# Scan and adapter mixture on one core: stores in rows over four units, a written order for every engine, 36 output slots

## The chip, the cores and the metric

One Trainium2 chip, one core. The metric is the device time of one execution in microseconds. Engines are named as in the profile: PE (TensorE matmul), PEld (its weight load), DVE (VectorE), ACT (ScalarE), POOL (GpSimd), SP (SyncE, which only issues DMAs here).

## What is computed

Inputs: a and b of 8 x 6400 x 128 (float32), gate weights 128 x 8, and eight adapters A (128 x 16) and B (16 x 128). First a scan over the 6400 steps of each of the 8 sequences, then on each of the 51200 rows a mixture of the two adapters with the largest gate logits:

```python
for t in range(S):
    h = a[:, t] * h + b[:, t]
    out[:, t] = h
...
logits = x @ w_gate
topk = np.argpartition(-logits, K, axis=1)[:, :K]
...
z = x[mask] @ A[e]
delta[mask] += w[mask, k, None] * (z @ B[e])
...
return x + delta
```

w is the softmax of the two selected logits. The output is 51200 x 128 float32, 26.2 MB, and a and b are 26.2 MB each.

## The kernel before

The 51200 rows are cut into 100 units of 512 rows. Loads bring two units of one input at a time (512 KB, 4 KB to a partition; four loads bring one), into a ring of eight slots for a and one for b. The slots of a are shifted by one unit, so that an a pair is units 1-2, 3-4 and so on, and a b pair 2-3, 4-5. For one unit, numbered v or w in the code:

- AB (PE): transposes of a into the bank pA (one buffer) and of b into pB (two), 64 x 64 pieces in float32; for units 0, 1 and 99 some of it in 128 x 128 pieces, as A and AB apart.
- aev (ACT): copies pA to a_st. scan (DVE): the scan along the free axis, from a_st and pB to xT in float16, a ring of 16 units. Sequences that begin within a unit cut a scan in two.
- L (PE): logits into a part of the bank pTL. Gating works on groups of one to four units: lev (ACT) copies the logits out, then m1, p1, p2, p3, m2, p4 to p7 (m1 and m2 on DVE, the others on GpSimd; the first three groups sort with max on DVE and may have p-steps there), and sig (ACT), which gives the weights g.
- Z (PE): x times all eight A, into pZ (two buffers). mul: the product of Z and g into zw, on DVE from PSUM or, at units 6, 10 and so on to 86, on GpSimd behind an evacuation zev by ACT.
- T (PE): transposes of zw into pTL, the bank of L. tev (ACT): evacuation to zwT.
- R (PE): x through an identity matrix into pO (two buffers), then D (PE): zwT times B on top. oev: evacuation to outt, on ACT, for the last ten units on ACT or DVE.
- st (SP): store from outt, a ring of 24 slots of one unit, two units at a time where these form a pair, so that a partition holds 8 consecutive rows, 4 KB. To get there, R and D take the x and zw of a pair in steps of 8 rows: `x_rows` reads every eighth column of xT, `evacuated` writes a tev with the rows of a pair dealt out. R of a pair therefore waits for both scans and D for both evacuations (`mates`). Units 0, 1 and 96 to 99 are stored singly in 2 KB rows.

The order on each engine is made in `_Plan.schedule`: a list scheduler at build time that goes through the operations by estimated costs and by keys (unit plus an offset by kind). A store is held until scan u0 + 22 (`HOLD`). In the DMA queue of SP, loads go by their unit, a and b in turn. An operation on a shared bank ("TL" of T, tev, L and lev; "A") waits for the last one of the other engine there. Seven matmuls on zeros (`heat`) run ahead of the first load, three more (`fill`) behind the first transposes.

Of the kernel before, what the change touches and what calls it, by code (L numbers as in the profile page):

```python
# [5 lines left out]
ALU = mybir.AluOpType  # L6
ACTF = mybir.ActivationFunctionType
F32 = mybir.dt.float32
# [4 lines left out]
KEY = {  # L13
    "AB": -228.9, "aev": 79.1, "scan": 140.1, "L": -12.2, "lev": -63.6, "gate": 83.5, "sig": 69.7, "Z": 27.8,
    "mul": -75.3, "zev": 6.2, "T": -117.7, "tev": 38.1, "R": 189.8, "D": 29.2, "oev": 168.4,
}
SLACK = {"pe": 20.0, "dve": 20.0, "act": 0.0, "pool": 60.0, "sp": 120.0}
# [3 lines left out]
POOL_MULS = (2, 10, 4, 2)  # L21
# [3 lines left out]
WIDE = 100  # L25
SOLO = (2, 4)
FUSE = (100, 100)
WIDE8 = 460.0
RING = 8
XR = 16  # L30
NOUT = 24
TAIL = 10
FILLS = 1


class _Op:


    def __init__(self, name, engs, kind, unit, cost, emit, deps, dma, bank, mode):
        self.name = name  # L40
        self.engs = engs
        self.eng = engs[0]
        self.kind = kind
        self.unit = unit
        self.cost = cost
        self.emit = emit
        self.deps = deps
        self.dma = dma
        self.bank = bank
        self.mode = mode  # L50
        self.signal = False
        self.done = None
# [7 lines left out]


# [30 lines left out]
class _Plan:  # L92


    def __init__(self, sems, offset, slack):
        self.sems = sems
        self.offset = offset
        self.slack = slack
        self.ops = {}
        self.order = {e: [] for e in sems}  # L100

    def add(self, name, eng, kind, unit, cost, emit, deps=(), dma=None, bank=None, mode=None):

        engs = (eng,) if isinstance(eng, str) else eng
        cost = cost if isinstance(cost, dict) else {e: cost for e in engs}
        self.ops[name] = _Op(name, engs, kind, unit, cost, emit, list(deps), dma, bank, mode)

    def schedule(self, first, link, landing, switch):
        ops = self.ops
        users = {n: [] for n in ops}  # L110
        left = {}
        for op in ops.values():
            op.deps = [ops[d] for d in dict.fromkeys(op.deps) if d in ops]
            left[op.name] = len(op.deps)
            op.key = op.unit + self.offset.get(op.kind, 0.0)
            op.quick = min(c[0] for c in op.cost.values())
        for op in ops.values():
            for d in op.deps:
                users[d.name].append(op)
        begin, end = {}, {}  # L120
        cand = {e: [] for e in self.sems}
        free = {e: first for e in self.sems}
        bank = {}
        mode = None
        for op in ops.values():
            if not left[op.name]:
                for e in op.engs:
                    cand[e].append((0.0, op))
        todo = len(ops)
        while todo:  # L130
            found, soonest = [], {}
            for e, c in cand.items():
                for x in c:
                    op = x[1]
                    t = max(free[e], x[0])
                    if op.bank:
                        for o in bank.get(op.bank, {}).values():
                            if o.eng != e:
                                t = max(t, end[o.name])
                    if op.mode and mode and op.mode != mode:  # L140
                        t = max(t, free[e] + switch)
                    t += op.cost[e][0] - op.quick
                    found.append((t, op, e, x))
                    if t < soonest.get(e, 1e18):
                        soonest[e] = t
            e0 = min(soonest, key=soonest.get)
            limit = soonest[e0] + self.slack.get(e0, 0.0)
            t, op, e, pick = min((f for f in found if f[2] == e0 and f[0] <= limit), key=lambda f: (f[1].key, f[0]))
            t -= op.cost[e][0] - op.quick
            for x in op.engs:  # L150
                cand[x].remove(pick)
            op.eng = e
            mode = op.mode or mode
            if op.bank:
                held = bank.setdefault(op.bank, {})
                op.deps += [o for o in held.values() if o.eng != e]
                held[e] = op
            self.order[e].append(op)
            begin[op.name] = t
            free[e] = t + op.cost[e][0]  # L160
            if op.dma:
                ready = free[e] + 1000.0
                wait = max(0.0, link - ready)
                link = max(link, ready) + op.dma[2]
                end[op.name] = link + 300.0 + min(wait, landing(link))
            else:
                end[op.name] = t + op.cost[e][1]
            todo -= 1
            for u in users[op.name]:
                left[u.name] -= 1  # L170
                if not left[u.name]:
                    for x in u.engs:
                        cand[x].append((max(end[d.name] for d in u.deps), u))
        self.begin, self.end = begin, end
        self.span = max(end.values())
        for op in ops.values():
            for d in op.deps:
                d.signal = True
        for e, seq in self.order.items():
            n = 0  # L180
            for op in seq:
                if op.dma:
                    op.done = op.dma[:2]
                else:
                    n += op.signal
                    op.done = (self.sems[e], n)
# [18 lines left out]
def bass_associative_scan_2x2__then__mixture_of_adapters_kernel(  # L205
# [20 lines left out]
    lo, hi, every, at = POOL_MULS  # L226
    ON_POOL = lambda v: lo < v < NU - hi and v % every == at
# [22 lines left out]
    with ExitStack() as stack:  # L250
# [15 lines left out]
        A_e = sb(nc.sbuf_tensor("A_e", [E, D * R], F32))  # L266
        xT = sb(nc.sbuf_tensor("xT", [128, XR * UT], F16))
        zw = [sb(nc.sbuf_tensor(f"zw{i}", [128, Q, 128], F16)) for i in range(2)]
        zwT = [sb(nc.sbuf_tensor(f"zwT{i}", [128, 2 * UT], F16)) for i in range(2)]
# [26 lines left out]
        s_cst = sb(nc.semaphore("s_cst"))  # L296
        dma_sem = {}

        plan = _Plan(sems, KEY, SLACK)
        add = plan.add  # L300

        def add_dma(name, eng, unit, starts, slot, time, deps=()):
# [11 lines left out]
            add(name, eng, "dma", unit, (450.0 * len(starts), 0.0), emit, deps, (sem, value, time))  # L314


        add("id0", "pool", "fix", -109, (200.0, 450.0), lambda h: h.memset(ident_f[:, :], 0.0))
# [3 lines left out]
            "fix",  # L321
            -109,
            (300.0, 400.0),
# [9 lines left out]
            ["id0"],  # L333
        )

        def cst_load(name, dst, src, after):

            sem = sb(nc.semaphore(f"s_{name}"))
            add(
                name,  # L340
                "act",
                "fix",
                -109,
                (450.0, 0.0),
                lambda h: h.dma_start(dst, src).then_inc(sem, 16),
                after,
                (sem, 16, 100.0),
            )
# [9 lines left out]
        add("w0", "dve", "fix", -109, (60.0, 200.0), lambda h: h.memset(warm[:, :], 0.0))  # L358
        add("table", "act", "fix", -108, (1500.0, 1600.0), lambda h: h.activation(warm[:, :], warm[:, :], ACTF.Sigmoid), ["w0"])
        add("wt", "dve", "fix", -109, (270.0, 400.0), lambda h: h.memset(warm_t[:, :], 0.0))  # L360
# [6 lines left out]
        add("heat", "pe", "fix", -109, (372.0 * HEATS, 372.0 * HEATS), heat, ["wt"], mode="half")  # L367

        def fill(w):


            def emit(h):
                for _ in range(3):
                    last = h.matmul(pO[1][:, :], warm_t[:, 0:128], warm_t[:, :])
                return last

            add(f"fill{w}", "pe", "fix", 1000.0, (600.0, 800.0), emit, [f"AB{w}"])

        for w in range(FILLS):
            fill(w)  # L380
        add("idh", "dve", "fix", -108, (150.0, 330.0), lambda h: h.tensor_copy(ident_h[:, :], ident_f[:, :]), ["id"])
        add("cstg", "pool", "fix", -108, (190.0, 290.0), lambda h: h.tensor_copy(wg_h, cst_f[:, 0:E]), ["ld_g"])
        add(
            "cstA",
            "pool",
            "fix",
            -107,
            (290.0, 390.0),
            lambda h: h.tensor_copy(Acat_h, cst_f[:, E : E + 128]),
            ["ld_A"],  # L390
        )
        add(
            "cstB",
            "pool",
            "fix",
            -106,
            (290.0, 390.0),
            lambda h: h.tensor_copy(Bcat_h, cst_f[:, E + 128 : E + 256]),
            ["ld_B"],
        )  # L400

# [525 lines left out]
```

## Time and profile before

| what | us |
|---|---|
| runs, median of 3 (lowest to highest) | 204.45 (204.28 to 204.6) |
| the profiled execution | 204.28 |
| its span, first to last instruction | 202.5 |
| PE busy | 191.0 |
| DVE busy | 184.7 |
| ACT busy | 174.0 |
| POOL busy | 115.7 |

The span is what the profile shows; 1.78 us of the execution lie around it. Matmuls are pipelined, so PE's busy time is not work at its peak; how long a stage of PE takes is read from start to start in its timeline. In a row of groups, the number behind x is the count, then busy time, mean ns of one, and the idle time just before with what ended it. A DMA row gives KB of one and the time from issue to landing. The granted clock of TensorE was 1.00 throughout.

### The profile page before, as it was taken

The page shows a single profiled execution, that of the slowest core. Times are in us where ns is not written, and L with a number is a line of the kernel's source. Part 1 is how long each engine was busy: PE and PEld are TensorE (multiplying, and loading weights), DVE is VectorE, ACT ScalarE, POOL GpSimd, SP SyncE. Part 2 cuts the span into 40 slices and gives each one's busy share as a digit, 9 for nine tenths or more (in the row PEclk, how much of TensorE's full clock was granted, in tenths as well). Part 3 has the DMA queues.
Part 4 walks back from the last instruction along what each step waited for, and adds up shares of the span by engine and source line. Part 5 has one row for each costly group of instructions (what it writes and reads, how often), then busy time and mean ns, then how long its engine had stood idle before and what let it go on. Part 6 is the DMA issues. An engine that isn't in the chain of part 4 may idle for free.

```text
span 202.5 us, 8763 instructions
## 1 busy us (share of the span) xinstructions
PE 191.0 (94%) x3594; PEld 171.4 (85%) x3594; DVE 184.7 (91%) x268; ACT 174.0 (86%) x383; POOL 115.7 (57%) x244
## 2 busy tenths in 40 slices
PE   7888988899999999999999999999999999999982
PEld 3666777789899999999999999999999999998981
DVE  1699989999999999999999999999999999988970
ACT  2366775969999999999999999999999999999882
POOL 1325337668467565656746656565674687865620
PEclk9999999999999999999999999999999999999999
DMA  7999999999999999999999999999999999988866
GB/s 185 401 408 409 406 408 406 403 406 411 403 413 414 410 419 409 409 411 414 412 416 409 414 413 411 411 415 415 409 412 414 413 414 410 385 350 350 324 271 263
DMA packets 23687, 79.35 MB, mean 392 GB/s; under 512 B 3680, under 2 KB 3808, under 8 KB 23648
## 3 DMA queue, kind: packets, MB, share of 16 engines
q1 hardware_dynamic: 22320, 78.65, 97.3%
q8 instruction: 29, 0.48, 1.0%
q10 hardware_dynamic: 1328, 0.14, 0.5%
q14 instruction: 10, 0.08, 0.1%
HBM read 52.56 MB, written 26.21 MB: 389 GB/s over the span
## 4 chain that ended last, share of the span: by engine, by line
PE 84%; ACT 6%; DVE 5%; issue 2%; POOL 1%; DVEq 0%
PE pA L86 27%; PE pO L82 23%; PE pTL L86 14%; PE pZ L82 10%; PE pTL L82 5%; DVE xT L510 4%; PE pB L86 4%; ACT a_st L491 2%; ACT outt L821 2%; PE pB L82 2%; ACT zwT L786 1%; DVE mx L589 1%; ACT Lg L583 0%; ACT z_sb L715 0%; POOL pn L632 0%
## 5 line engine op out<-in xcount | busy, mean ns | idle before, releaser
L510 DVE TENSOR_TENSOR_SCAN xT<-a_st,xT,pB 128x512 f16<-128x512 f32 x96 | 120.1, 1251 | 3.2 <-ACT zwT L786 0.5
L491 ACT COPY a_st<-pA 128x512 f32<-128x512 f32 x100 | 60.6, 606 | 19.2 <-PE pB L86 14.6
L86 PE MATMUL pA<-ident_f,a_in 64*128 64x64 f32 (+1 forms) x792 | 71.8, 230 | 2.5 <-ACT a_st L491 0.7
L86 PE MATMUL pB<-ident_f,b_in 64*128 64x64 f32 (+1 forms) x792 | 71.9, 230 | 0.3 <-issue 0.2
L86 PEld LDWEIGHTS pA<-ident_f,a_in 64*128 64x128 f32 (+1 forms) x792 | 57.9, 139 | 10.9 <-ACT a_st L491 1.9
L821 ACT COPY outt<-pO 128x512 f32<-128x512 f32 x96 | 59.5, 626 | 1.9 <-PE pO L82 1.7
L786 ACT COPY zwT<-pTL 128x512 f16<-128x512 f16 x95 | 58.4, 615 | 1.0 <-PE pTL L86 1.0
L86 PEld LDWEIGHTS pB<-ident_f,b_in 64*128 64x128 f32 (+1 forms) x792 | 57.5, 138 | 1.0 <-issue 0.7
L729 DVE TENSOR_TENSOR zw<-pZ,g 128x512 f16<-128x512 f32 x79 | 53.2, 679 | 2.4 <-PE pTL L86 1.4
L82 PE MATMUL pO<-ident_h,xT 128*128 128x128 f16 x400 | 40.8, 227 | 0.9 <-ACT outt L821 0.9
L86 PE MATMUL pTL<-ident_h,zw 128*128 128x128 f16 x380 | 37.8, 221 | 0.5 <-ACT zwT L786 0.4
L82 PE MATMUL pZ<-cst_h,xT 128*128 128x128 f16 x400 | 38.1, 219 | 0.0
L82 PE MATMUL pO<-cst_h,zwT 128*128 128x128 f16 x400 | 36.8, 218 | 0.5 <-ACT zwT L786 0.4
L82 PEld LDWEIGHTS pO<-ident_h,xT 128*128 128x128 f16 x400 | 32.5, 147 | 1.5 <-ACT outt L821 1.2
L729 POOL TENSOR_TENSOR zw<-z_sb,g 128x512 f16<-128x512 f32 x21 | 22.3, 1060 | 17.8 <-PE pTL L82 17.3
L82 PE MATMUL pTL<-cst_h,xT 128*128 128x8 f16 x400 | 27.5, 174 | 1.4 <-DVE xT L510 1.3
L82 PEld LDWEIGHTS pZ<-cst_h,xT 128*128 128x128 f16 x400 | 27.8, 114 | 0.1
L86 PEld LDWEIGHTS pTL<-ident_h,zw 128*128 128x128 f16 x380 | 21.8, 98 | 6.7 <-ACT zwT L786 0.5
L625 POOL TENSOR_TENSOR d<-Lg,m 128x128 f32<-128x128 f32 (+3 forms) x29 | 10.7, 369 | 26.6 <-DVE m L618 26.5
L82 PEld LDWEIGHTS pTL<-cst_h,xT 128*128 128x128 f16 x400 | 23.5, 117 | 2.6 <-DVE xT L510 2.0
L82 PEld LDWEIGHTS pO<-cst_h,zwT 128*128 128x128 f16 x400 | 23.8, 98 | 1.0 <-PE pO L82 0.9
L660 POOL TENSOR_SCALAR pn<-d 128x128 f32<-128x128 f32 (+3 forms) x31 | 17.3, 557 | 2.7
(38 smaller groups left out, 138.3 us busy)
## 6 DMA issues: line engine op xcount, KB each, us to landing
a_in<-in_a_dram SPq DMA_DIRECT2D x49, 512.0 KB, 14.4
b_in<-in_b_dram SPq DMA_DIRECT2D x49, 512.0 KB, 14.2
out_dram<-outt SPq DMA_DIRECT2D x47, 512.0 KB, 13.9
out_dram<-outt SPq DMA_DIRECT2D x6, 256.0 KB, 3.0
a_in<-in_a_dram SPq DMA_DIRECT2D x2, 256.0 KB, 9.1
b_in<-in_b_dram SPq DMA_DIRECT2D x2, 256.0 KB, 4.1
cst_f<-in_moe_A_dram ACTq DMA_DIRECT2D x1, 64.0 KB, 4.2
cst_f<-in_moe_B_dram ACTq DMA_DIRECT2D x1, 64.0 KB, 4.9
```

Of the source, the lines that this page charges most:

```text
L82: return self.h.matmul(*args, **kw)
L86: return self.h.transpose(*args)
L491: lambda h: h.copy(a_st[w % 2][:, :], pA[0][:, :]),
L510: last = h.tensor_tensor_scan(out=x_at(lo, hi), data0=a_st[w % 2][:, lo:hi], data1=pB[w % 2][:, lo:hi], initial=init, op0=ALU.mult, op1=AL ...
L589: last = h.max(mx[s][:, j, :], Lg[s][:, j, :])
L625: lambda h: h.tensor_tensor(out=v(d1[s]), in0=v(Lg[s]), in1=bc(m1[s]), op=ALU.subtract),
L660: lambda h: h.tensor_scalar(v(pn[s]), v(d2[s]), 0.0, -1.0e30, ALU.is_lt, ALU.mult),
L729: lambda h: h.tensor_tensor(out=oview, in0=zview, in1=gview, op=ALU.mult),
L786: lambda h: h.copy(*evacuated(v)),
L821: return copy(outt[:, v % NOUT, :], pO[v % NO][:, :])
```

## The change

The scheduler, its costs and its keys go out. `ORDERS` holds one letter for each operation of each engine, `BANKS` the order on the two shared banks; a letter takes the next unit of its kind. `ELSE` names the operations that leave the engine first named for them. Stores of units 8 to 87 take four units, 16 rows or 8 KB to a partition, those of 2 to 7 and 88 to 95 two, the others one. R and D of four units then wait for four scans and four evacuations; zwT holds four units per buffer, xT 20 units and outt 36. The products on GpSimd are at the same 21 units. The three `fill` matmuls are gone. Unused branches (`WIDE`, `FUSE`, `A_e`) go out too.

```diff
-KEY = {
...
+CODES = dict(
+    zip(
+        "bdfkpqrvhyBCEijAacsLZuTtRDozlx41567gm23nwe",
+        "idz id ld_g ld_A ld_B w table wt heat idh cstg cstA cstB lda ldb A AB aev scan L Z mul T tev R D oev zev lev mx p4 p1 p5 p6 p7 sig m1 p2 p3 m2 st end".split(),
+    )
+)
+ORDERS = {
+    "pe": """
+        hAaAaLaLRaZZaLRLaZTLaaZDTLaLaZTDLaLRaTZRaDaZLTLLaRDLaZTLaDLZRaTZDaTLRLaZDRLaDTRaTZaZLTLLaZRLTaZLTDDa
+        ZTLRZaDRTLDaRLTZaZTDRaDLTZRLLaRDTZaZTDRaLDTRZaRLTLDZaLTRZDaTDRZaTRDZDaLRZLTaDRLTLZaZTDRaDTLLZRaDTZRa
...
+        RTaZDRTLLaZDRTaDRTZDaTLLZRaZTDRaDLTRaDRZLLTLDARZDRTDZRZTDRaDRTTDZZRLLRDDTZTRZDRTZDTRZDRTDRZDTRZDRTDT
+        RDRD
+    """,
+    "dve": """
+        qvyssx165sxsusxsus6msusmnsusnmsusnsusmsusnsusmsusnsusmususnsusumsusnsusmususnsusmususnsusumsusnsusmu
...
+        munssnuumsusmnsumsunsusmnsusnsumuunusuumouunuuouuo
+    """,
+    "act": """
+        fkpcclclrcgclcgcltcolgctctclocgtccozgctlgctococtcotlcgzoctcotcltcgtcztocotcotlcgtoctozcoltctoctogcot
...
+    "sp": """
+        ijijjjijjijjiiiijijjiijijjjiijjiijjiijiwiiwwjjjwijiiiijjwwjiiwjijjwwiwjjwijijijijijijiijjiiiwjjijiwij
+        jwjjwjiwjiiiijwwwjjwiiwwwwwwwwwwwwwe
+    """,
 }
...
+ELSE = "oev90 oev94 oev97 p1_0 p5_0 p6_0 p6_2".split()
...
-XR = 16
-NOUT = 24
+PAIRS = (2, 96)
+QUADS = (8, 88)
+XR = 20
+NOUT = 36
...
+        def length(v):
+            return 4 if QUADS[0] <= v < QUADS[1] else 2 if PAIRS[0] <= v < PAIRS[1] else 1
 
         def mates(v):
-            return [v] if v in solo else [v // 2 * 2, v // 2 * 2 + 1]
+            n = length(v)
+            return list(range(v // n * n, v // n * n + n))
...
         def x_rows(v, q):
...
+            n = length(v)
+            x0 = (v // n * n) % XR * UT
+            return xT[:, x0 : x0 + n * UT].rearrange("d (m i) -> d i m", i=n * Q)[:, v % n * Q + q, :]
...
-                [f"T{v}"] + [f"D{w}" for w in mates(v - 4)],
+                [f"T{v}"] + [f"D{w}" for m in mates(v) for w in mates(m - 8)],
...
+            n = max(length(u), 2 if u < NU - SINGLE else 1)
+            stores.append((u, n))
+            u += n
...
-        plan.schedule(700.0, 3000.0, lambda t: 400.0, 94.0)
+        plan.arrange()
```

In the letters of SP, i is a load of a, j a load of b and w a store; in those of PE, a is AB and A the a part of a unit that is transposed apart.

More of the change, by code (lines that the diff above doesn't have):

```diff
@@ L92, with __init__ @@
 class _Plan:
-    def __init__(self, sems, offset, slack):
+    def __init__(self, sems):
         self.sems = sems
-        self.offset = offset
-        self.slack = slack
         self.ops = {}
[L100 to L176, printed above, removed]
@@ new lines, in add, with pick, arrange @@
+    def add(self, name, eng, emit, deps=(), dma=None, bank=None):
+        if not isinstance(eng, str):
+            eng = eng[name in ELSE]
+        self.ops[name] = _Op(name, eng, emit, list(deps), dma, bank)
+    def pick(self, codes, ops):
+        queue = {}
+        for op in ops:
+            queue.setdefault(op.base, []).append(op)
+        got = [queue[CODES[c]].pop(0) for c in "".join(codes.split())]
+        assert not any(queue.values())
+        return got
+    def arrange(self):
+        ops = list(self.ops.values())
+        for op in ops:
+            op.deps = [self.ops[d] for d in dict.fromkeys(op.deps) if d in self.ops]
+        self.order = {e: self.pick(ORDERS[e], [op for op in ops if op.eng == e]) for e in self.sems}
+        for name, codes in BANKS.items():
+            held = {}
+            for op in self.pick(codes, [op for op in ops if op.bank == name]):
+                op.deps += [o for e, o in held.items() if e != op.eng]
+                held[op.eng] = op
+        for op in ops:
@@ L225, in bass_associative_scan_2x2__then__mixture_of_adapters_kernel @@
     NZ, NO = 2, 2
-    lo, hi, every, at = POOL_MULS
-    ON_POOL = lambda v: lo < v < NU - hi and v % every == at
+    ON_POOL = lambda v: v in POOL_MULS
     def cut(sizes_head, size, sizes_tail):
@@ L312, in emit @@
                 return last
-            add(name, eng, "dma", unit, (450.0 * len(starts), 0.0), emit, deps, (sem, value, time))
-        add("id0", "pool", "fix", -109, (200.0, 450.0), lambda h: h.memset(ident_f[:, :], 0.0))
+            add(name, eng, emit, deps, (sem, value))
+        add("idz", "pool", lambda h: h.memset(ident_f[:, :], 0.0))
         add(
@@ L365, in heat @@
             return last
[L367 to L400, printed above, removed]
+        add("heat", "pe", heat, ["wt"])
+        add("idh", "dve", lambda h: h.tensor_copy(ident_h[:, :], ident_f[:, :]), ["id"])
+        add("cstg", "pool", lambda h: h.tensor_copy(wg_h, cst_f[:, 0:E]), ["ld_g"])
+        add("cstA", "pool", lambda h: h.tensor_copy(Acat_h, cst_f[:, E : E + 128]), ["ld_A"])
+        add("cstB", "pool", lambda h: h.tensor_copy(Bcat_h, cst_f[:, E + 128 : E + 256]), ["ld_B"])
         rings = {"a": a_in, "b": b_in}
         rows_of = {"a": a.rearrange("b s d -> (b s) d"), "b": b.rearrange("b s d -> (b s) d")}
-        solo = set(range(SOLO[0])) | set(range(NU - SOLO[1], NU))
+        def length(v):
+            return 4 if QUADS[0] <= v < QUADS[1] else 2 if PAIRS[0] <= v < PAIRS[1] else 1
         def mates(v):
-            return [v] if v in solo else [v // 2 * 2, v // 2 * 2 + 1]
+            n = length(v)
+            return list(range(v // n * n, v // n * n + n))
         alone = {("a", 0), ("b", 0), ("b", 1), ("a", NU - 1)}
@@ L477, in transposes @@
                 both = [x for pair in zip(pa, pb) for x in pair]
-                add(f"AB{w}", "pe", "AB", w, (548.0, 750.0), emit(both), deps + [load_of["a", w], load_of["b", w]], mode="half")
+                add(f"AB{w}", "pe", emit(both), deps + [load_of["a", w], load_of["b", w]])
             else:
                 for t, name, steps, first in (("a", f"A{w}", pa, []), ("b", f"AB{w}", pb, [f"A{w}"])):
-                    mode = "full" if (t, w) in alone else "half"
-                    add(name, "pe", "AB", w, (500.0, 700.0), emit(steps), deps + [load_of[t, w]] + first, mode=mode)
+                    add(name, "pe", emit(steps), deps + [load_of[t, w]] + first)
         def a_evac(w):
@@ L546, in emit @@
                 return last
-            add(f"L{v}", "pe", "L", v, (126.0, 310.0), emit, [scanned(v), f"lev{k - 1}", "cstg"], bank="TL", mode="full")
+            add(f"L{v}", "pe", emit, [scanned(v), f"lev{k - 1}", "cstg"], bank="TL")
         def gating(k):
@@ L569, in bc, with step @@
                 return t[:, 0:c].to_broadcast([128, c, E])
-            def step(name, eng, time, emit, deps):
-                if isinstance(time, str):
-                    time = cost(time)
-                    time = {e: time[e] for e in ((ge,) if isinstance(ge, str) else ge)}
-                add(f"{name}_{k}", eng, "gate", u, time, emit, deps)
+            def step(name, eng, emit, deps):
+                add(f"{name}_{k}", eng, emit, deps)
             add(
@@ L692, in emit, with fill @@
                 return last
-            deps = [scanned(v), f"mul{v - NZ}", f"zev{v - NZ}", "cstA"]
-            add(f"Z{v}", "pe", "Z", v, (223.0, 423.0), emit, deps, mode="full")
+            free = [f"mul{v - NZ}", f"zev{v - NZ}"]
+            if v in FILL:
+                def fill(h):
+                    for _ in range(3 if v == 0 else 1):
+                        last = h.matmul(pZ[v % NZ][:, :], warm_t[:, 0:128], warm_t[:, :])
+                    return last
+                add(f"F{v}", "pe", fill, free + ["wt"])
+            add(f"Z{v}", "pe", emit, [scanned(v), "cstA", f"F{v}"] + free)
         pool_muls = [v for v in range(NU) if ON_POOL(v)]
@@ L791, in delta, with emit @@
         def delta(v):
-            def emit(what):
+            def emit(left, right, first):
                 def run(h):
-                    for q, w in [(q, w) for q in range(Q) for w in what]:
-                        left, right = {"x": (x_rows(v, q), ident_h[:, :]), "d": (zw_rows(v, q), Bcat_h)}[w]
+                    for q in range(Q):
                         last = h.matmul(
                             pO[v % NO][:, q * 128 : (q + 1) * 128],
-                            left,
+                            left(v, q),
                             right,
-                            start=w == "x" and q == 0,
-                            stop=w == "d",
+                            start=first and q == 0,
+                            stop=not first,
                             skip_group_check=True,
@@ L808, in delta @@
             deps = [f"scan{mates(v)[-1]}", f"oev{v - NO}", "idh"]
[L809 to L810 removed]
             tevs = [f"tev{w}" for w in mates(v)]
[L812 to L816 removed]
+            add(f"R{v}", "pe", emit(x_rows, ident_h[:, :], True), deps)
+            add(f"D{v}", "pe", emit(zw_rows, Bcat_h, False), [f"R{v}", "cstB"] + tevs)
         def o_evac(v):
@@ L842, in store @@
             s0 = u0 % NOUT
-            rows = out[u0 * UT : (u0 + n) * UT, :].rearrange("(p i) d -> p (i d)", p=128)
+            rows = out[u0 * UT : (u0 + n) * UT, :]
+            dst, src = rows.rearrange("(n p i) d -> p n (i d)", p=128, i=Q), outt[:, s0 : s0 + n, :]
+            if length(u0) == n > 1:
+                dst, src = rows.rearrange("(p i) d -> p (i d)", p=128), src.rearrange("p n c -> p (n c)")
             add_dma(
@@ L846, in store @@
                 "sp",
-                u0 + HOLD,
-                [(rows, outt[:, s0 : s0 + n, :].rearrange("p n c -> p (n c)"))],
+                [(dst, src)],
                 ("o", s0, n),
-                1.036 * ((625.0 if n == 2 else 650.0) * n + 13.0),
                 [f"oev{v}" for v in range(u0, u0 + n)] + [f"scan{u0 + HOLD}"] * (u0 + HOLD < FREE),
```

192 lines of the change are left out of this document (56 added, 136 removed).

## The prediction

> **What bounds the kernel now.** I read the page first, then windows by stage, then the timelines of single engines.
>
> ```profile
> span 202.5 us, 8763 instructions
> PE 191.0 (94%) x3594; PEld 171.4 (85%) x3594; DVE 184.7 (91%) x268; ACT 174.0 (86%) x383; POOL 115.7 (57%) x244
> DMA  7999999999999999999999999999999999988866
> ```
>
> Three things are near full at once: PE, DVE and the DMA engines. The windows say which of them limits in which stage (columns: length, busy time of PE, PEld, DVE, ACT and POOL with their instructions, granted clock, DMA share, GB/s).
>
> ```profile
> 10.00:25.00 15.00, 12.86 (x247) 10.80 (x244) 14.75 (x34) 10.02 (x27) 5.69 (x21) 1.00 1.03 407
> 25.00:45.00 20.00, 17.75 (x341) 15.34 (x338) 18.95 (x25) 14.79 (x33) 11.45 (x22) 1.00 1.03 406
> 55.00:165.00 110.00, 110.00 (x2195) 101.70 (x2192) 107.75 (x142) 105.11 (x229) 69.30 (x124) 1.00 1.03 412
> 175.00:185.00 10.00, 9.89 (x187) 9.06 (x185) 8.90 (x15) 9.38 (x22) 6.43 (x18) 1.00 0.93 371
> 185.00:195.00 10.00, 9.84 (x161) 9.44 (x159) 9.17 (x16) 8.72 (x21) 5.91 (x14) 1.00 0.73 286
> 199.20:200.80 1.60, 0.00 (x0) 0.00 (x0) 0.00 (x0) 0.00 (x0) 0.00 (x0) 1.00 1.03 385
> ```
>
> From 10 to 25 us DVE is busy 14.75 of 15 us while PE has 2.1 us free: the scans set the pace. From 55 to 165 PE is busy all of 110 us and DVE has 2.25 us free. After 175 no engine is full: DVE alone is idle 1.93 us of 20, and the DMA engines fall to a share of 0.73, so stores then wait for results and not results for stores. That PE is really full in the middle shows in its timeline, one unit long:
>
> ```profile
> 99.84 0.40 PE L86 MATMUL pTL<-ident_h,zw 128*128 128x128 f16 x4
> 100.08 0.27 PE L82 MATMUL pTL<-cst_h,xT 128*128 128x8 f16 x4
> 100.20 0.38 PE L82 MATMUL pO<-cst_h,zwT 128*128 128x128 f16 x4
> 100.42 0.39 PE L82 MATMUL pZ<-cst_h,xT 128*128 128x128 f16 x4
> 100.65 0.42 PE L82 MATMUL pO<-ident_h,xT 128*128 128x128 f16 x4
> 101.00 0.27 PE L86 MATMUL pA<-ident_f,a_in 64*128 64x64 f32 x1
> ...
> 101.65 0.40 PE L86 MATMUL pTL<-ident_h,zw 128*128 128x128 f16 x4
> ```
>
> Order T, L, D, Z, R, AB, one after the other with no idle note; the next T begins 1.81 us after the last. From start to start D takes 0.22, Z 0.23, and R 0.35, of which some 0.09 is the change over to AB (its four matmuls keep D's rhythm otherwise), so R alone is 0.26. One hundred such units are 181 us, and PE has the same matmuls after the change, three warm-up matmuls less. So the middle can't gain by order; only the start, where PE waits for DVE, and the end can.
>
> **The change, part by part.** The sum is made against this execution's 204.28 us: its span of 202.5 and 1.78 around it. The median of the runs, 204.45, is 0.17 more.
>
> *Loads at the start.* SyncE's new order puts the loads of b 4-5 ahead of a 3-4, of b 6-7 and 8-9 ahead of a 5-6. Counted in 256 KB, a 5-6 ends at the 17th piece in place of the 13th. Before, the load that ended at the 13th (a 5-6 itself, issued 4.03) and that at the 17th (a 7-8, issued 4.98) landed so, and unit 5 ran so:
>
> ```profile
> 4.03 0.43 SPq L311 DMA_DIRECT2D a_in<-in_a_dram  x1
> a_in<-in_a_dram SPq DMA_DIRECT2D x1, 512.0 KB, 8.3
> 4.98 0.43 SPq L311 DMA_DIRECT2D a_in<-in_a_dram  x1
> a_in<-in_a_dram SPq DMA_DIRECT2D x1, 512.0 KB, 11.2
> 13.44 0.24 PE L86 MATMUL pA<-ident_f,a_in 64*128 64x64 f32 x1 [0.24 <-ACT a_st L491]
> 14.75 0.67 DVE L729 TENSOR_TENSOR zw<-pZ,g 128x512 f16<-128x512 f32 x1
> 15.89 1.26 DVE L510 TENSOR_TENSOR_SCAN xT<-a_st,xT,pB 128x512 f16<-128x512 f32 x1
> ```
>
> 4.03 + 8.3 is 12.3, 4.98 + 11.2 is 16.2. AB of unit 5 began at 13.44; now it can't before 16.2, 2.8 later. Its scan began 2.45 after AB, of which the product at 14.75 and the sort behind it took 1.1; with 1.6 from AB to scan it now begins at 17.8, 1.9 late. Behind it on DVE stand all later scans and products, and PE, ACT and GpSimd wait for those. Bounds: 2.3 if nothing is caught up (the product of unit 1, 0.67 less what else moves ahead of that scan, also falls behind it), and 0 if the 17th piece comes 1.3 us sooner, as four pieces at 407 GB/s (2.6 us after 12.3) would give, and the 1.05 us that DVE has free from 25 to 45 takes the rest. I take **+1.2**.
>
> *Small steps at the start.* Four small gate steps stand on DVE in both kernels, other ones. Unit 0's p5 and p6 now wait on DVE for GpSimd's p4, with scan 2 behind them; against that, scan 1 goes ahead of the first sort. ACT's table load now stands between the evacuations of a for units 2 and 3:
>
> ```profile
> L359 ACT ACT_TABLE_LOAD x1 | 1.3, 1283 | 2.3 <-issue 2.3
> ```
>
> It is hidden while unit 3 waits for its a, which comes one load later than before; uncovered it is 1.3. Three warm-up matmuls go; PE was idle around them. The rest is 0.2 to 0.3 us each and points both ways: **0** (bounds -0.3 and +1.3).
>
> *PE's backlog.* A store row over four units asks that R of a unit waits for all four scans and D for all four evacuations. When AB of unit 24 begins (46.6 us) the old order has done this (pZ: 60/4 = 15 Z; zwT: 40/4 = 10 D; pO: 91 less 40 less 3 warm-ups, 12 R):
>
> ```profile
> 0.00:46.40 46.40, 5.55 (x60) 4.04 (x60) 7.30 (x11) 1.25 (x3) 1.00 0.99 382
> 0.00:46.40 46.40, 3.19 (x40) 2.33 (x40) 7.06 (x12) 1.00 0.99 382
> 0.00:46.40 46.40, 8.68 (x91) 6.26 (x91) 0.00 (x0) 5.89 (x10) 1.00 0.99 382
> ```
>
> Read off the new order, it is 14 Z, 8 D, 10 R: one Z, two D, two R fewer, 0.23 + 0.44 + 0.52 = 1.2 us of matmuls moved out of a stage where PE had time into the one where it has none. Ahead of the last AB the new order does one T and one R more than the old, 0.24 + 0.26 = 0.5. **+1.7** by the last AB (bounds +0.5, if DVE's free time takes up the first part, and +1.7).
>
> *The end.* The old end:
>
> ```profile
> 184.62 0.61 PE L86 MATMUL pA<-ident_f,a_in 128*128 128x128 f32 x4
> 187.22 1.28 DVE L510 TENSOR_TENSOR_SCAN xT<-a_st,xT,pB 128x512 f16<-128x512 f32 x1
> 196.91 0.69 DVE L821 COPY outt<-pO 128x512 f32<-128x512 f32 x1 [0.36 <-PE pO L82]
> 198.57 0.58 ACT L821 COPY outt<-pO 128x512 f32<-128x512 f32 x1 [0.16 <-PE pO L82]
> out_dram<-outt SPq DMA_DIRECT2D x1, 256.0 KB, 2.4
> ```
>
> From 187.2 DVE carries the end: scan 99, eight products, four evacuations. One of these moves to ACT: 0.69 less. And a 99 is now transposed and evacuated ahead of AB 99, so scan 99 needs only b's part and needn't come 2.6 us after; I count 1.2 of that. **-1.9** (bounds -0.7 and -3.8, with all of DVE's 1.93 idle gone).
>
> *An order without a cycle.* In the old order nearly every unit is the same six steps; in the new one hardly two units are alike, with L twice in one unit and missing in the next. T and L share a bank with ACT's reads, so PE's next T or L waits for the evacuation ahead of it. The old cover from L to the next T is 1.4 us (D, Z, R, AB) for an evacuation of 0.59 that begins as L ends; in the new order some thirty places between units 20 and 90 have 1.2.
>
> ```profile
> 100.43 0.59 ACT L786 COPY zwT<-pTL 128x512 f16<-128x512 f16 x1
> PE pTL L86 <- ACT zwT L786: 0.4, 1, 0.4
> ```
>
> Before, PE waited for this once. A wait on PE holds every matmul behind it. Bounds 0 and 30 x 0.4 = 12; most covers still exceed the need by 0.3, so I take **+0.4**.
>
> *8 KB store rows, 36 slots.* On the path: **0**. The trace has 2 KB rows at 385 GB/s (the last stores) and 4 KB rows at 412, none of 8 KB. The 21 MB of stores take 51 us of DMA time at 412; 7% to either side is 3.4 us, and the free share after 175 (0.07 and 0.27 of 10 us each) covers it; uncovered it would be 3.4. The last four units are stored singly as before. Bounds -0.3 and +0.7.
>
> *Reading xT for R.* Weights of R are now read every 16th element, not every 8th. The rows for steps of 8, 4 and 1:
>
> ```profile
> L82 PEld LDWEIGHTS pO<-ident_h,xT 128*128 128x128 f16 x400 | 32.5, 147 | 1.5 <-ACT outt L821 1.2
> L82 PEld LDWEIGHTS pZ<-cst_h,xT 128*128 128x128 f16 x400 | 27.8, 114 | 0.1
> L82 PEld LDWEIGHTS pO<-cst_h,zwT 128*128 128x128 f16 x400 | 23.8, 98 | 1.0 <-PE pO L82 0.9
> ```
>
> The step costs: +16 ns for 4, +49 for 8. Carried on it would be some +110 for 16, so +60 ns on 320 matmuls, 19 us, all on PE; the other bound is 0, if a step of 8 already has the worst of it. R's matmuls stand 10 ns further apart than D's (0.26 and 0.22 for four) though their weights take 49 ns longer, so I take **0** and keep 19 us as a rival. [...]
>
> **Sum:** 1.2 + 0 + 1.7 - 1.9 + 0.4 = +1.4: span 203.9, execution 205.7, against the median **205.8 us**, slower by 0.7%.
>
> **Rivals.**
> *Faster by the end.* One mechanism: after 175 us DVE's gaps close, because the new order has its products further ahead. Price: all of the 3.8, with the backlog at its low bound of 0.5 and load order and irregular order at 0: -3.3, 201.2; half of it 202.8. For it: DVE is idle 1.93 of 20 us there. Against it: once start and middle have lost more than 3.3 us, it is no gain.
>
> *No change.* Head and end cancel: 204.4. PE's 181 us in the middle speak for it.
> *R's weights.* 205.8 + 19, about 225, if a step of 16 costs as the rows carried on.
> *A load too late in the middle.* The load of a 59-60 now stands on SyncE behind the store of units 28 to 31, which waits for scan 50; scan 5 ended 3.7 us after its AB began, so of nine units at 1.81 us (16.3) 12.6 are left.
>
> ```profile
> a_in<-in_a_dram SPq DMA_DIRECT2D x49, 512.0 KB, 14.4
> ```
>
> At the median landing it is 1.8 late: 207.6. Against it: with loads issued later, fewer stand in the queue ahead of it.
>
> **How the numbers follow.** What can be told from no change is 0.2%, 0.4 us: 204.0 to 204.9. Forecast (204.9 to 207) 0.38, late load 0.07, R's weights 0.06; faster 0.40; no change 0.09. So faster 0.40, same 0.09, slower 0.51. The forecast's own range is 204.9 to 207.5. The whole goes down to 201.4 (the faster rival nearly in full) and up to 209 (the late load with the dearer bounds of start and order), leaving out the weights and some of each edge.
>
> **What would show it.** Start: AB of unit 5 at about 16.3 us and DVE with 1 to 2 us more idle before 25. Middle: PE with waits on zwT between 55 and 165, or none; R's weight loads at 147 ns or well above. End: first of the last transposes to last store under 17.9 us; DVE with three evacuations. I am wrong if AB 24 begins by 46.6 us or sooner, or if DVE's idle time after 175 falls under 1 us.

## The result and the profile after

The changed kernel takes 209.99 us (median of 4 runs, 209.08 to 210.79) against 204.52 for the kernel before: 2.7% slower, ratio 1.0268 with a 95% interval of 1.0217 to 1.0319. The forecast was 205.8. Medians here are of all runs, while ratios leave out slow ones, over 1.5% above the fastest of their kernel. The profiled execution took 209.08 us, with a span of 207.3, so the difference to explain in the traces is 207.3 - 202.5 = 4.8 us of span.

The page of the changed kernel: span, share by engine, granted clock and DMA share in 40 slices of 5.2 us.

```profile
span 207.3 us, 8761 instructions
PE 194.7 (94%) x3591; PEld 174.4 (84%) x3591; DVE 183.9 (89%) x267; ACT 178.1 (86%) x385; POOL 115.8 (56%) x244
PEclk9998569999999999999999999999999999999999
DMA  6999999999999799999999999999999999975996
```

The fifth and sixth slice show what the page of before doesn't have: PE at half its clock. The windows of the stages (columns as in the prediction):

```profile
10.00:25.00 15.00, 10.77 (x173) 9.08 (x171) 11.82 (x29) 8.06 (x20) 4.72 (x18) 0.82 1.03 409
15.00:20.00 5.00, 2.20 (x45) 1.81 (x43) 4.10 (x14) 1.84 (x6) 1.81 (x6) 0.96 1.02 403
20.00:25.00 5.00, 4.54 (x58) 4.04 (x56) 3.34 (x5) 2.83 (x7) 0.75 (x4) 0.50 1.03 410
25.00:45.00 20.00, 19.15 (x348) 17.03 (x346) 18.77 (x25) 15.00 (x35) 12.04 (x29) 0.88 1.03 406
55.00:165.00 110.00, 109.46 (x2145) 99.82 (x2140) 105.39 (x138) 105.52 (x224) 67.28 (x120) 1.00 1.01 398
175.00:185.00 10.00, 10.00 (x202) 9.13 (x199) 9.92 (x16) 9.90 (x25) 7.71 (x20) 1.00 0.94 382
185.00:195.00 10.00, 10.00 (x180) 9.71 (x178) 9.00 (x16) 9.50 (x23) 6.60 (x16) 1.00 0.69 281
```

From 10 to 25 us both engines lose: PE does 10.77 us (12.86 before) and DVE 11.82 (14.75 before). A clock of 0.96, 0.50 and 0.88 in stretches of 5, 5 and 20 us is half clock for 0.4 + 5 + 4.8 = 10.2 us; the clock record in the trace has 0.50 from 19.6 to 29.8 and 1.00 on both sides. In the middle PE is again busy nearly always, but gets 2145 matmuls done where it did 2195. From 175 us on PE has no gap at all.

What PE waited for stands in its timeline and in the DMA view of single issues:

```profile
16.18 0.22 PE L119 MATMUL pB<-ident_f,b_in 64*128 64x64 f32 x1
19.05 0.24 PE L119 MATMUL pA<-ident_f,a_in 64*128 64x64 f32 x1 [2.64 <-DVE d L563]
```

```profile
6.10 1.85 SPq L287 DMA_DIRECT2D a_in<-in_a_dram  x4
a_in<-in_a_dram SPq DMA_DIRECT2D x1, 512.0 KB, 12.8
4.67 0.43 SPq L287 DMA_DIRECT2D a_in<-in_a_dram  x1
a_in<-in_a_dram SPq DMA_DIRECT2D x1, 512.0 KB, 9.2
```

AB of unit 7 begins 2.64 us after PE's last matmul. The timeline names a gate step on DVE; but the load of a 7-8, issued at 6.10, landed 12.8 later, at 18.9, 0.1 us before AB 7 begins: where the engine named had long been done, it was the DMA. In the kernel before a 7-8 landed at 16.2 and AB 7 began at 17.3. The load of a 5-6, on which the prediction built, was issued at 4.67 and landed at 13.9.

To see where the 4.8 us arise I count for each kernel the PE time lost up to a moment: the time passed, less the work that PE has done by then, each step at its uncovered length start to start (AB 0.74 with the change over to it, R 0.257, T and Z 0.224, D 0.221, L 0.130; warm-up matmuls count as nothing).

| PE time lost by | 30 us | 45 us | 185 us | end of span |
|---|---|---|---|---|
| before | 12.1 | 14.1 | 16.1 | 22.9 |
| after | 16.2 | 17.6 | 22.1 | 27.7 |
| e1_loads | 12.7 | 14.2 | 17.1 | 22.7 |
| e2_fill | 13.8 | 15.8 | 20.0 | 26.7 |

So the change loses 3.5 us by 45 us, 2.5 more from 45 to 185 (4.5 against 2.0), and gains 1.2 behind that.

### The profile page after: what moved, and what is told of

It reads as the page before. It is cut to its first block, busy times and chain, and to the rows that moved or that the text cites. A ratio compares the mean times of both kernels' runs of the same rounds, so it can differ in the third digit from the quotient of the medians.

```text
span 207.3 us, 8761 instructions
## 1 busy us (share of the span) xinstructions
PE 194.7 (94%) x3591; PEld 174.4 (84%) x3591; DVE 183.9 (89%) x267; ACT 178.1 (86%) x385; POOL 115.8 (56%) x244
## 4 chain that ended last, share of the span: by engine, by line
PE 87%; ACT 4%; DMA 3%; issue 2%; DVE 2%; SPq 1%
PE pA L119 27%; PE pO L115 25%; PE pZ L115 12%; PE pTL L119 12%; PE pTL L115 6%; PE pB L119 4%; DMA b_in<-in_b_dram 3%; ACT a_st L414 1%; DVE xT L433 1%; ACT zwT L663 1%; SPq L287 1%; ACT outt L692 1%; ACT L322 1%; ACT Lg L488 0%; DVE zw L614 0%
## 5 line engine op out<-in xcount | busy, mean ns | idle before, releaser
L119 PE MATMUL pA<-ident_f,a_in 64*128 64x64 f32 (+1 forms) x792 | 73.7, 234 | 5.9 <-DVE d L563 2.6
L119 PE MATMUL pB<-ident_f,b_in 64*128 64x64 f32 (+1 forms) x792 | 73.8, 234 | 0.3
L119 PEld LDWEIGHTS pB<-ident_f,b_in 64*128 64x128 f32 (+1 forms) x792 | 58.9, 142 | 1.3 <-PE pA L119 0.7
L663 ACT COPY zwT<-pTL 128x512 f16<-128x512 f16 x95 | 56.7, 597 | 3.0 <-PE pTL L115 2.0
L115 PE MATMUL pO<-ident_h,xT 128*128 128x128 f16 x400 | 42.9, 231 | 0.2 <-issue 0.2
L115 PE MATMUL pO<-cst_h,zwT 128*128 128x128 f16 x400 | 39.1, 221 | 0.2 <-ACT zwT L663 0.2
L115 PEld LDWEIGHTS pO<-cst_h,zwT 128*128 128x128 f16 x400 | 25.4, 99 | 2.2 <-PE pO L115 0.5
L115 PE MATMUL pTL<-cst_h,xT 128*128 128x8 f16 x400 | 25.4, 174 | 0.4 <-issue 0.2
L119 PEld LDWEIGHTS pTL<-ident_h,zw 128*128 128x128 f16 x380 | 24.3, 99 | 1.6 <-issue 0.3
L115 PEld LDWEIGHTS pTL<-cst_h,xT 128*128 128x128 f16 x400 | 21.9, 117 | 1.9 <-DVE xT L433 0.3
## 6 DMA issues: line engine op xcount, KB each, us to landing
out_dram<-outt SPq DMA_DIRECT2D x20, 1024.0 KB, 12.1
```

The lines of the kernel that those rows point to most:

```text
L115: return self.h.matmul(*args, **kw)
L119: return self.h.transpose(*args)
L663: lambda h: h.copy(*evacuated(v)),
```

## The experiments

All ratios are to the kernel before, run on the same chip, with 95% intervals.

**e1_loads: the load order alone undone.**

```diff
-        ijijjijjijjiiiijijjiijijjjiijjiijjiijiwiiwwjjjwijiiiijjwwjiiwjijjwwiwjjwijijijijijijiijjiiiwjjijiwij
+        ijijjijijijijijiijjiijijjjiijjiijjiijiwiiwwjjjwijiiiijjwwjiiwjijjwwiwjjwijijijijijijiijjiiiwjjijiwij
```

> The changed kernel with its first 17 loads back in the order of before (a and b in turn, so a 7-8 is the tenth load and not the twelfth); all else, the later loads too, as changed. Theory 'start': the 2.6 us that PE waits ahead of AB 7 go, the granted clock stays at 1.0 from 5 us on, the PE time lost by 30 us falls from 16.2 to 13 or less, and the time from 210.0 to 206 to 207. Rival 'gates': what delays the start is the other order of gate steps, products and transposes around it; then AB 7 comes sooner but AB 12 is still over 3 us later than before, and the time falls by less than 1 us.

Measured: 204.25 us, ratio 1.0001 (0.9980 to 1.0022). All of the loss is gone, 5.7 us for the order of a few loads, more than 'start' expected (206 to 207). The clock clause of the theory fell: in the profiled run, which took 204.11, PE waited 0.94 us ahead of unit 1, and the windows from 5 to 15 us have half clock for 2.4 + 2.5 + 1.9 = 6.8 us.

```profile
6.73 0.24 PE L119 MATMUL pA<-ident_f,a_in 64*128 64x64 f32 x1 [0.94 <-DMA a_in<-in_a_dram]
```
```profile
5.00:10.00 5.00, 3.75 (x39) 3.06 (x39) 2.64 (x6) 1.43 (x4) 0.00 (x0) 0.76 1.04 402
10.00:12.50 2.50, 2.50 (x32) 2.11 (x32) 2.05 (x10) 2.47 (x6) 0.93 (x4) 0.50 1.02 408
12.50:15.00 2.50, 2.50 (x42) 2.11 (x41) 2.21 (x3) 1.03 (x4) 1.36 (x6) 0.62 1.02 406
```

**e8, e9, e10: a 7-8 alone, as the 10th, 11th and 13th load** (12th as changed). A run of letters that is moved, and for the 13th a swap:

```diff
-        ijijjijjijjiiiiji
+        ijijjijjiijjiiiji   (e8)
+        ijijjijjijijiiiji   (e9)
...
```
```diff
+        sp = self.order["sp"]
+        sp[11], sp[12] = sp[12], sp[11]
```

> The changed kernel with one load moved: a 7-8 ahead of b 8-9 and b 10-11, so that it is the tenth load again, as before; a 5-6 stays behind b 6-7. Theory 'a 7-8': this one load is the cause; AB 7 begins by 17.8 us, and the time falls to 204 to 206. Rival 'a 5-6': the prediction's load (a 5-6, one load later) starts the delay, DVE never recovers, and the time stays over 207.

> The changed kernel with a 7-8 one load sooner: eleventh, behind b 8-9 and ahead of b 10-11 (tenth in e8_a7_first, 204.4 us; twelfth as changed, 210.0). It should land between 15.1 (as tenth) and 18.9 (as twelfth), at about 17.3, so that PE waits some 1 us ahead of AB 7. Theory 'a 7-8, then the clock': the clock stays at 1.0 behind so short a wait, and the time is 204.5 to 206. Rival 'each load later costs the same': half way, 207 to 207.5.

> The changed kernel with a 7-8 one load later still: thirteenth, behind a 9-10. It should land some 1.3 us later, at about 20.2 (512 KB at 407 GB/s). Theory 'late load': every microsecond that AB 7 begins later is paid, 211 to 212. Rival 'only the clock': the dip is there already, a wait of 3.9 us costs no more than one of 2.6, and the time stays within 0.6 us of 210.0.

| a 7-8 as load no. | landed | AB 7 begins | us | ratio |
|---|---|---|---|---|
| 10 (e8) | 15.1 | 17.23 | 204.38 | 0.9985 (0.9969 to 1.0001) |
| 11 (e9) | 16.3 | 17.52 | 204.11 | 0.9993 (0.9971 to 1.0016) |
| 12 (as changed) | 18.9 | 19.05 | 209.99 | 1.0268 (1.0217 to 1.0319) |
| 13 (e10) | 20.0 | 20.15 | 211.51 | 1.0331 (1.0281 to 1.0382) |

One load is the cause, and the curve has a step. e8 came out as 'a 7-8' expected. In e9 the load is hidden (AB 7 begins 1.2 us after it landed), and e9's two expectations are both missed on the good side. e10's time is the one expected of 'late load', but not by its mechanism: by 45 us it has lost only 0.2 us more than the changed kernel (17.8), and 1.7 goes at one later place (below). The step is higher than a load: from the 11th to the 12th the landing moves by 2.6 us, where a load takes 1.3. The trace's completion times of the 16 DMA engines show why. In the changed kernel the load ahead of a 7-8 is complete on all 16 between 16.0 and 16.4; a 7-8 is complete on 15 of them by 17.7, and on the last one at 18.9. In the loads behind it, too, the last engine is some 1.3 us behind the other 15. The DMA view of 15 to 16 us has the reason:

```profile
q1 hardware_dynamic: 111, 0.39, 97.6%
q8 instruction: 1, 0.02, 6.4%
```

One packet of instructions (it begins at 15.9 us), 6.4% of 16 engines for 1 us, is 1.0 us on one engine. That it ran on the engine that is late isn't recorded; in the kernel before, too, the loads with one late engine begin right behind this packet. In the profile of before it stands between 14 and 15 us (6.5%); a 7-8 already was the first load behind it there, complete on 15 engines by 14.9 and on the last one at 16.2, with 1.1 us to spare.

**e2_fill: PE kept busy while it waits.**

```diff
-        hAaAaLaLRaZZaLRLaZTLaaZDTLaLaZ
+        hAaAaLaLRaZZaLRLaZTLaFaZDTLaLaZ
...
+        def fill(h):
+            for _ in range(8):
+                last = h.matmul(pB[1][:, :], warm_t[:, 0:128], warm_t[:, :])
+            return last
+        add("fill7", "pe", fill, ["scan5"])
```

> The changed kernel, same orders, with eight more warm-up matmuls (results unused) on PE ahead of AB 7, where it waits for a 7-8. Theory 'clock': the loss is half clock from 19.6 to 29.8 us and not the late load itself; with PE kept at work the granted clock stays at 1.0 and the time falls by 1.5 to 2.5 us, to about 208. Rival 'late load': DVE sets the pace there anyway, the clock reads 1.0, and the time stays within 0.5 us of 210.0.

Measured: 208.01 us, 1.0172 (1.0154 to 1.0191), as 'clock' expected. AB 7 begins no sooner, at 19.35, but from 20 us on the windows show the full clock, and DVE without a gap from 25 to 45:

```profile
20.00:25.00 5.00, 4.55 (x94) 4.16 (x92) 4.23 (x6) 3.96 (x9) 1.34 (x5) 1.00 1.03 410
25.00:45.00 20.00, 18.60 (x364) 16.51 (x364) 20.00 (x29) 16.14 (x38) 13.52 (x31) 1.00 1.03 406
```

(The profiled run has a dip of its own, half clock from 8.9 to 12.3 us.) By 45 us PE has lost 1.8 us less than in the changed kernel. So of the 5.5 us about 2 go with the half clock, and 3.5 remain: the late load with what follows from it. The split is rough, since the eight matmuls also move the ends of PE's code parts (below).

**e6_before_loads and e11_before_fill: the late load alone, in the planner's order.**

```diff
+        late = "a0 b0 a1 b1 b2 a3 b4 b6 a5 b8 b10 a7 a9 a11 a13 b12 a15 b14".split()
+        self.order["sp"][:18] = [ops[f"ld{x}"] for x in late]
+        ops["fill7"] = _Op("fill7", ("pe",), "fix", 0, {"pe": (0.0, 0.0)}, self.keep, [ops["scan5"]], None, None, None)   (e11)
+        self.order["pe"].insert(self.order["pe"].index(ops["AB7"]), ops["fill7"])   (e11)
```

> The kernel before, its planner's orders kept, but its first 18 loads issued in the changed kernel's order (a 7-8 as the twelfth load). Theory 'start': AB 7 waits for a 7-8, to about 18.9 us in place of 17.3; at least that 1.6 us is lost, with a dip of the granted clock more: 206 to 209. Rival 'taken up': DVE's queue ahead (scan 7 begins at 18.74, product and sort before it) hides it, 204.4 to 205.0.

> The kernel before with its first 18 loads in the changed order (e6_before_loads, 207.3 us at a clock of 0.975 to 0.983) and eight warm-up matmuls on PE ahead of AB 7. Theory 'clock': the granted clock stays over 0.99 and 1 to 2 us of the 2.7 come back, 205.3 to 206.3. Rival 'late load': 206.8 or more.

Measured: e6 207.29 us, 1.0150 (1.0127 to 1.0173), as 'start' expected; e11 209.19, 1.0214 (1.0187 to 1.0241). The load order slows the kernel before too, by 2.7 us, with this wait:

```profile
19.16 0.34 PE L86 MATMUL pA<-ident_f,a_in 64*128 64x64 f32 x1 [1.51 <-DMA a_in<-in_a_dram]
```

e11 missed 'clock'; it lies over 206.8, as 'late load' expected, but 1.9 us over e6 as well. Its clock is 1.00 from 20 to 45 us, yet by 30 us both have lost 14.1 us of PE time. That isn't a clean test of the clock: e11's eight matmuls run until 19.96, so AB 7 begins 0.8 us later than in e6, and its profiled run has half clock from 14.2 to 17.6 us. What the half clock costs in this order stays open. The 1.9 us over e6 come at the end, where the last stores landed 4 us after issue and not 2.3; whether the eight matmuls did that stays open.

**e3_pairs, e7_pairs_loads, e4_quads_plan: the stores.**

```diff
-QUADS = (8, 88)
+QUADS = (100, 100)   (e3, e7; each of these 20 stores then is two)
```
```diff
-SOLO = (2, 4)
-XR = 16
-NOUT = 24
+PAIRS = (2, 96)
+QUADS = (8, 88)
+XR = 20
+NOUT = 36
```

The second is e4: the kernel before, planner and all, with these sizes and the functions length, mates, zw_tile, evacuated and x_rows of the change.

> The changed kernel's written orders, slots and xT, but units 8 to 87 stored in pairs (4 KB rows), two stores where one stood, held for the same scan; R then waits for two scans, D for two evacuations. Theory 'order': the 2.0 us of PE time lost between 45 and 165 us come from the order on PE, so the time stays at 209.5 to 210.3. Rival 'four units': they come from D's and R's wait for four units or from the larger stores, and the time falls to about 208.

> e1_loads with units 8 to 87 stored in pairs (as in e3_pairs). Theory 'order': stores of four units cost nothing in the written order, so this is the time of e1_loads, 203.9 to 204.7. Rival 'four units': the waits of R and D for four units cost some of the PE time lost in the middle (3.0 us between 45 and 165 us in e1_loads, 1.7 before), so this is 0.5 to 1.3 us faster, 203.0 to 203.6.

> The kernel before with its planner and its POOL products, and of the change only the stores of units 8 to 87 in 8 KB rows, xT of 20 units, zwT of four and 36 slots. Theory 'order': the stores cost nothing, the planner again finds a regular order, 204.0 to 205.0. Rival 'four units': waits for four units or the 8 KB rows cost 1 us or more, 205.5 to 207.

Measured: e3 209.07 us, 1.0218 (1.0175 to 1.0260), between its two expectations and not to be told from the changed kernel; e7 205.10, 1.0028 (1.0018 to 1.0037), slower than both its expectations, against 1.0001 (0.9980 to 1.0022) with stores of four: in the written order 8 KB rows cost nothing, and may save some 0.3%. e4 took 221.89, 1.0846 (1.0831 to 1.0861), a miss of 16 us for both theories. The same stores under the planner's old weights lose PE time all along, some 17 us by 60 and 27.1 by 165 (before: 15.0 and 15.8), and the last AB begins at 199.9 us. So stores of four are free in the written order and were dear under the planner. Which of e4's waits does it was not settled: no group of them in its list is over 2.2 us.

**e5_loads_fill, e12_a7_fill: the three warm-up matmuls put back** behind unit 0, in e1 and e8.

```diff
-        hAaAaLaLRa
+        hAaFAaLaLRa
...
+        add("fill0", "pe", fill, ["AB0"])   (three matmuls into pO[1])
```

> The changed kernel with its first 17 loads in the order of before and the three warm-up matmuls back on PE behind the transposes of unit 0. In e1_loads, without them, PE was idle for 0.94 us at 5.8 us, the granted clock fell to 0.5 from 7.5 to 14 us in the profiled run, and the runs went from 203.9 us (clock 1.0) to 207.9 (0.967). Theory 'clock': all runs now show a mean clock over 0.99 and 203.7 to 204.2 us, a spread under 0.7 us. Rival: the spread of e1_loads has another source; then it stays at 2 us or more.

> e8_a7_first (a 7-8 as the tenth load) with the three warm-up matmuls back behind the transposes of unit 0. In the profile of e8_a7_first the clock fell once, to 0.6 in the slice from 20 us on. Theory 'clock': runs at 0.99 or more and 203.7 to 204.2, faster than before by 0.2 to 0.4%. Rival: another gap than that one lets the clock fall, and the time stays at 204.2 to 204.6.

Measured: 205.54 us, 1.0015 (0.9993 to 1.0038), and 205.27 us, 1.0022 (0.9996 to 1.0049). Their profiled runs have the full clock and took 204.07 and 203.91, but others of their runs show a mean clock of 0.96 to 0.98 and 205.6 to 209.6 us. Keeping PE busy at that one place doesn't hold the clock from run to run. Theory 'clock' missed in both; e5's rival, another source of the spread, came true (204.1 to 209.6 us), e12's time missed its rival too, and what sets the clock stays open.

**e13 to e16: the ends of PE's code parts.** PE's code stands in 29 parts with a branch from each to the next. Between 45 and 185 us there are 22 or 23 such ends. Against the usual distances of the same matmuls, the changed kernel loses 2.7 us around them (1.7 before, 1.8 in e1, 4.9 in e10), at places where no engine is late. The same step, from L of unit 36 on, in the changed kernel and in e10:

```profile
77.08 0.19 PE L115 MATMUL pTL<-cst_h,xT 128*128 128x8 f16 x1 [0.23 <-issue]
```
```profile
79.09 0.19 PE L115 MATMUL pTL<-cst_h,xT 128*128 128x8 f16 x1 [1.52 <-issue]
```

The trace shows what goes with it, in the branches and in the packets of PE's code (q8 on the page: 29 packets of instructions, as many as parts, 0.48 MB in all; in the changed kernel each is 16 KB and takes 0.96 to 1.22 us). At this step the packet ended 0.2 us before the branch began (75.7 and 75.9 us), and the branch took 0.99 us. In e10 the packet ended at 77.4, after the branch had begun (76.7), and the branch took 2.29. Three more branches of the changed kernel in this stretch take 0.57 us or more, and there, too, the packet ended less than 1 us before; in e1 each packet ended 1.0 us or more before, and no branch takes over 0.5. Why these packets came later isn't shown.

The experiments end a part early, inside an AB (in e9, the changed kernel, e2 and the kernel before):

```diff
+    def cut(self):
+        if self.size - self.used < ROOM:
+            self.used = self.size
...
+                        if k == 9:
+                            h.cut()
```

> e9_a7_eleventh (204.1 us) with the ends of PE's code parts moved: a part now ends behind the ninth matmul of an AB where fewer than 84 of its 243 places are left (34 parts in place of 29). Theory 'code': a stop in the middle of an AB costs little (0.0 us at most of the ends that lay there), so the 1.4 us lost at the ends between 45 and 185 us fall under 0.7, and the time to 203.2 to 203.8, faster than both kernels. Rival 'order': the stops stay at the same steps of the order, 203.9 to 204.4; or the five more parts cost what is gained.

> The changed kernel with the same rule for the ends of PE's code parts. Theory 'code': of the 4.5 us of PE time lost between 45 and 185 us some 1.5 to 2 go, 208.0 to 208.7. Rival 'order': the loss there stays over 4, 209.5 to 210.5.

> e2_fill (eight warm-up matmuls ahead of AB 7, 208.0 us) with the same rule for the ends of PE's code parts. If the half clock from 19.6 to 29.8 us costs 2 us by itself, this is 2 us under e14_after_cuts, 206 to 206.7; if e2's gain came from the parts' moved ends, it is within 0.7 us of e14_after_cuts.

> The kernel before with the same rule. Its parts' ends cost 1.2 us between 45 and 185 us. Theory 'code': 203.6 to 204.3. Rival: the ends that cost are few and others take their place, 204.4 to 204.9.

Measured: 276.74, 275.50, 271.60 and 282.50 us; ratios 1.3529, 1.3447, 1.3162, 1.3785. All expectations missed by some 65 us and more, so these four don't tell the shares they were made for. They show another thing: PE stands still where no engine holds it, and by the packets it waits for its own code. The waits of e13 that no engine ended (total, count, longest):

```profile
PE pTL L120 <- issue: 14.7, 4, 5.4
PE pO L120 <- issue: 12.2, 3, 5.7
PE pB L124 <- issue: 12.1, 5, 4.5
PE pA L124 <- issue: 7.3, 5, 2.8
PE pTL L124 <- issue: 6.5, 1, 6.5
```

These are 18 waits and 52.8 us of the 73 by which e13's span is longer than e9's; its granted clock, 0.87 on average, will have part of the rest. They don't stand at the ends of the parts, where the branch mostly takes 0.18 us, but inside the parts. All but the shortest end 1.3 to 1.5 us after a packet of PE's code has ended. So with parts that end short the code itself seems to come late, at places that the edit didn't choose and for up to 6.5 us inside a part. That PE waits for the packet is read from these times; how its code is brought in was not shown.

## Why the prediction was wrong

**The step that failed: loads at the start, +1.2 with bounds of 0 to 2.3.** The place was nearly right, but SyncE's list was read wrongly and one load too short. It says "i j i j j i j j i j j i": a 3-4 stays ahead of b 4-5, a 5-6 moves by one load (it landed at 13.9, not at the 16.2 forecast; AB 5 began at 14.03), and a 7-8, which the working used only as a yardstick, moves by two. That load had 1.1 us to spare in the profile of before, and two loads are 2.6. Undone alone (e8) the move gives back 5.6 us, where the step had +1.2. That the sign came out right is in part luck: the load that the step priced, a 5-6, stays one load late in e8 too, and e8 loses nothing. The upper bound of 2.3 assumed that a late load costs at most its lateness. In the runs DVE ran dry behind it (11.82 of 15 us), PE's clock halved behind the wait (about 2 us, e2), and the later stops between code parts grew (1.8 us in e1, 2.7 as changed, where code packets came late). How the rest of the 5.6 us divides was not measured.

**No rival had the clock.** The row of before read 1.00 everywhere, and nothing in the text asked what a wait of some us would do to it.

**PE's backlog, +1.7.** The count of the letters was right, but work put off was not time lost. With the load back (e1) AB 24 begins at 45.1 us, sooner than before (46.6), and the loss by 45 us is 14.2 against 14.1.

**The end, -1.9.** PE time regained behind 185 us is 1.2, inside its bounds, but not by the mechanism named. DVE does three evacuations, as forecast, and still:

```profile
191.98 1.27 DVE L433 TENSOR_TENSOR_SCAN xT<-a_st,xT,pB 128x512 f16<-128x512 f32 x1
201.57 0.69 DVE L692 COPY outt<-pO 128x512 f32<-128x512 f32 x1 [0.28 <-PE pO L115]
```

From scan 99 to the end are 207.3 - 192.0 = 15.3 us, as before (202.5 - 187.2). The part of a 99 is transposed ahead, as forecast, but PE comes to b's part 3.4 us later (191.2 after 187.9; before 186.5 after 184.6), so scan 99 was not brought forward. PE carries the end: busy 10.00 of 10 us twice in the rows above. The prediction's own rows had 9.89 and 9.84 there, and it took DVE for the limit. The sign "first of the last transposes to last store under 17.9 us" was missed, at 19.4.

**The order without a cycle, +0.4.** PE loses 2.5 us more than before between 45 and 185, and 0.9 more with the load restored (e1). Hardly any of it is the wait for the bank that the step described; some 1.0 of the 2.5 sits at the ends of code parts, the rest is spread and not explained.

**What held.** Stores in 8 KB rows at 0 (e7 against e1). R's weights at a step of 16, 0 and not 19 us: 148 ns against 147. That a step of 8 already has the worst of it was the author's estimate, and the 1 ns between steps of 8 and 16 bears it out.

```profile
L115 PEld LDWEIGHTS pO<-ident_h,xT 128*128 128x128 f16 x400 | 33.2, 148 | 1.5 <-issue 0.4 <-ACT outt L692 0.2
```

No load is late in the middle: from unit 24 to 96 each has landed at least 4 us before its AB begins. AB 24 began at 48.8, later than 46.6, as forecast, but by way of another load.

## What to carry to other kernels

Before costing a new order of loads, list for every load how long it lay landed before its first use, and count the loads that move ahead of each one down to the last whose slack is under the shift; the tight one may be two further on. Here a late load at the start cost more than its lateness (5.9 us of time for 2.6 us of landing, from the 11th place to the 12th): DVE ran dry behind it, and PE's clock stood at a half for 10.2 us. And PE with 9.84 of 10 us busy turned out as good as full here: gaps on another engine there may be its shadow.

## What the runs showed of the hardware

PE's granted clock fell to a half after waits of 2.64 us (as changed) and of 0.94 us (e1), and stayed there for 10.2 us (19.6 to 29.8) and 6.8 us although PE was at work (4.54 of 5 us from 20 us on, as changed). The length of a wait doesn't settle it: early waits of 0.42 and 0.54 us were followed by 3.4 us of half clock in e9, and waits of 0.32 and 0.55 us at the same places by none in the changed kernel. What sets the clock was not shown.

PE waited for a 7-8 until the last of 16 DMA engines had done its share (18.9 us; 15 were done by 17.7). From the packet of PE's code on, which takes 1.0 us of one engine, eight loads in a row (seven in the kernel before) were complete on the last engine 1.2 to 1.4 us later than on the other 15.
